# Attention and two expert layers on one core: the first expert of layer one chosen from two batches, its first two blocks in a fixed order, and an earlier split of the last w2 parts

## The chip, the cores and the metric

One core of a Trainium2 chip runs the kernel. The core has a matrix engine (TensorE, PE in the profile, with its weight loads as PEld), VectorE (DVE), ScalarE (ACT), GpSimd (POOL) and SyncE (SP). Each runs its own instructions in order and waits for the others on semaphores. SP issues the transfers of weights and the transposing transfers, POOL the gathers and scatters by a list of rows (SPq and POOLq in the profile are these issues). The metric is device time in microseconds (us).

## The reference, cut to what matters

The inputs are q, k, v of 4 batches, 12 heads, 448 tokens, head size 64. First comes causal attention; its output is laid out as 1792 rows of 768. Then two layers of 8 experts, each of which sends a token to one expert:

```python
scores = where(causal_mask, -1e9, scale * q @ k.T)
x = (softmax(scores) @ v).transpose(0, 2, 1, 3).reshape(1792, 768)
# layer one: router on normalised rows
logits = (x / norm(x)) @ (emb / norm(emb)).T / tau
e = argmax(logits); gate = softmax(logits)[e]
x = gate * (relu(x @ w1[e]) @ w2[e])          # w1[e]: 768 x 1024, w2[e]: 1024 x 768
# layer two: router with a bias by the token's modality
logits = x @ w_gate + modality_bias[modality_id]
e = argmax(logits); gate = softmax(logits)[e]
out = gate * (relu(x @ w1b[e]) @ w2b[e])
```

Counted by this reference on its own inputs (seed 0), layer one sends to its experts 0 to 7: [1 319 229 126 542 464 87 24] tokens in all, [0 54 217 121 1 41 0 14] of them in the first batch and [0 317 217 124 106 45 73 14] in the first two. Layer two sends [869 3 0 0 0 0 920 0].

## The kernel before, in words

**Attention.** A loop over 24 pairs of heads (`for g in range(NPR + 3)`) runs as a pipeline: in iteration g the scores and exponents of pair g, the halves of pair g-1 (two f16 parts, transposed by DMA into the tiles th and tl), the values and the output xb of pair g-2 (`values`, `combine`), and the router products of pair g-3 (`route_t` transposes xb on PE, `route_l` multiplies it with the embeddings). Six pairs make a batch. When a batch is through, its rows go to memory (`store_x`) and its routing runs piece by piece (`route1`, advanced by `tick`): logits, argmax, a token's slot among its expert's, the gate, and a scatter of the tokens' records (`meta1`).

**The experts.** A layer's tokens are worked off in blocks of 128 of one expert. A block gathers its records (`gather_m`, tile mg), its rows (`gather_x`, tile xg), turns x (`prep`), multiplies with w1 (`up`, two halves n=0 and 1), applies relu, turns h, multiplies with w2 (`down`), and scatters its output. All of it is float32 made of two parts, a high part (w1h, w2h, xh, hh, casts on ACT) and the rest (w1l, w2l, xl, hl, subtractions on DVE), with three products of parts for each: an up half is 18 matmuls 128x512, a down 24 pairs of 128x384. An expert's weights come as six w1 and eight w2 pieces (w1r, w2r) and are split by `split_w`. Layer one has 18 blocks and layer two 16 by the counts above. Experts are taken in an order that `Lead.order` makes of the counts; `table` makes the list of blocks, `switches` the list of the blocks at which the expert changes.

**The lead.** The first expert of layer one is chosen while attention still runs, so that its weights arrive and are split early: `choose(cnt1)` takes the expert with the most tokens so far. Before, this happens after batch 0 (expert 2, 217 tokens). `check` then sets flags: `full[0]`, at least 128 of its tokens are in the first two batches, so that block 0 can be gathered early, and `full[1]`, at least 256 in three batches, for block 1. `load_lead(m1, 1, c)` loads one piece of its w1 in each iteration from 18 on (`LEAD`). By the counts `full[0]` is set and `full[1]` is not.

**The opening of layer one.** `open_phase` and `first_block` run block 0 while the last batch's routing (`last_route1`) is finished in steps between the matmuls; then `run` works off the sections, j = 1 to 21, where section j holds up of block j and down of block j-1. Blocks 0, 1 and 2 turn x on PE (`prep`, j < FIRSTQ), later ones on DVE (`x_squares`, then `prep`). `warm` issues six matmuls whose result nobody reads, in front of the opening.

**The end.** In layer two block 15 is the last and the only one of its expert. After down of block 14, `split_w(2)` splits all eight w2 pieces of that expert, and `down_last` computes the two halves of the output, each sent away by itself.

The order of the instructions on every engine is that in which the Python program emits them; nothing reorders them later.

## Time and profile before

| | us |
|---|---|
| median of 3 timed runs | 921.35 |
| lowest and highest of them | 916.38, 922.5 |
| the profiled execution | 910.5 |
| its span in the trace | 908.7 |
| mean granted clock of TensorE, as a share of full speed | 0.98 |

All times in the trace count from the span's start. Attention's products end at 243.34, layer one's block 0 begins its up at 246.50, and section 3 (the first that works alike in both kernels) begins at 309.97. The last matmul is issued at 900.25. A row of a timeline gives the start and the duration of one instruction, or of several that follow one another (x6), the engine, the line in the program, the output and the inputs, and in brackets how long the engine stood idle before it and what released it. A matmul's duration contains its way through the pipeline: the next one starts earlier than this one ends.

### The profile page before, as it was taken

What the parts mean: (1) busy time and instruction counts of PE and PEld (TensorE: products, weight loads), DVE (VectorE), ACT (ScalarE), POOL (GpSimd) and SP (SyncE); (2) the same over time, 40 slices, a digit from 0 to 9 for tenths busy, and PEclk for the clock granted to TensorE, in tenths of its full rate; (3) what the DMA queues carried; (4) which work ended last, traced back from release to release, by engine and by line L of the source; (5) the groups of instructions that cost most, each with busy time, mean ns of one, the idle gap of its engine ahead of it and who ended that gap; (6) DMA issues with size and microseconds to landing.
All of it is one profiled execution on the core that took longest, in us unless ns stands there. A gap on an engine that the chain in (4) does not pass through costs nothing. (4 is left out here: it accounts for less than half of the span.)

```text
span 908.7 us, 21165 instructions
## 1 busy us (share of the span) xinstructions
PE 859.1 (95%) x7010; PEld 753.3 (83%) x7010; DVE 699.3 (77%) x1798; ACT 427.8 (47%) x779; POOL 478.0 (53%) x477
## 2 busy tenths in 40 slices
PE   4999999999789899999999999999999999999995
PEld 3877877877577899998898999888899898898984
DVE  7899999999785766787936884468886678976793
ACT  3676777767434664575525652245112133312323
POOL 7877577875255255454444564431653544544531
PEclk9999999999899999999999999999999999999998
DMA  6799996979717765578515662120281233511110
GB/s 193 161 154 171 203 181 159 210 172 218 241 53 254 278 257 176 203 282 296 193 38 183 201 231 97 53 76 6 57 332 39 67 88 133 185 48 54 54 38 16
DMA packets 114456, 137.46 MB, mean 151 GB/s; under 512 B 78382, under 2 KB 82788, under 8 KB 114289
## 3 DMA queue, kind: packets, MB, share of 16 engines
q1 hardware_dynamic: 101376, 108.76, 44.1%
q0 software_dynamic: 12912, 26.83, 9.4%
q8 instruction: 61, 1.00, 0.5%
q14 instruction: 107, 0.87, 0.3%
HBM read 101.48 MB, written 19.92 MB: 134 GB/s over the span
## 5 line engine op out<-in xcount | busy, mean ns | idle before, releaser
L765 POOL DMA_INDIRECT xg<-x,xi x128 | 137.7, 1076 | 98.3 <-DMA x<-yb,mg 50.8
L974 PE MATMUL h<-w1h,xh 128*128 128x512 f32 x408 | 165.0, 404 | 1.0 <-ACT xh L958 1.0
L976 PE MATMUL h<-w1h,xl 128*128 128x512 f32 x408 | 161.5, 396 | 1.0 <-DVE xl L959 1.0
L975 PE MATMUL h<-w1l,xh 128*128 128x512 f32 x408 | 161.3, 395 | 0.2 <-DVE w1l L715 0.2
L1039 PE MATMUL o<-w2h,hh 128*128 128x384 f32 x528 | 138.3, 343 | 0.2 <-ACT hh L988 0.2
L1039 PE MATMUL o<-w2h,hl 128*128 128x384 f32 x528 | 136.7, 340 | 0.9 <-DVE hl L989 0.9
L1039 PE MATMUL o<-w2l,hh 128*128 128x384 f32 x528 | 136.0, 339 | 0.1
L1016 DVE STREAM_TRANSPOSE hs<-h 32x256 f32<-32x256 f32 x240 | 107.0, 446 | 14.3 <-PE h L976 9.0
L435 ACT ACTIVATE ex<-sc,nm 112x112 f32<-112x112 f32 (+1 forms) x192 | 83.8, 503 | 62.2 <-DVE nm L430 60.9
L1039 PEld LDWEIGHTS o<-w2h,hl 128*128 128x128 f32 x528 | 96.4, 190 | 1.2 <-DVE hl L989 1.2
L1039 PEld LDWEIGHTS o<-w2l,hh 128*128 128x128 f32 x528 | 96.1, 189 | 0.7 <-DVEq L1330 0.4
L1039 PEld LDWEIGHTS o<-w2h,hh 128*128 128x128 f32 x528 | 94.8, 190 | 1.8 <-ACT hh L988 0.4
L976 PEld LDWEIGHTS h<-w1h,xl 128*128 128x128 f32 x408 | 77.3, 190 | 19.6 <-DVE xl L959 2.0
L1022 ACT ACTIVATE hh<-hs 128x512 fp32r<-128x512 f32 x30 | 18.4, 631 | 158.1 <-PE o L1039 88.6
L974 PEld LDWEIGHTS h<-w1h,xh 128*128 128x128 f32 x408 | 77.5, 190 | 16.6 <-ACT xh L958 1.1
L975 PEld LDWEIGHTS h<-w1l,xh 128*128 128x128 f32 x408 | 77.5, 190 | 16.2 <-DVE w1l L715 1.0
L715 DVE TENSOR_TENSOR w1l<-w1r,w1h 128x1024 fp32r<-128x1024 f32 x66 | 76.5, 1221 | 8.3 <-ACT w1h L713 7.5
L430 DVE TENSOR_REDUCE nm<-sc 112x1 f32<-112x112 f32 (+1 forms) x192 | 75.6, 439 | 6.1 <-PE sc L425 5.0
L715 DVE TENSOR_TENSOR w2l<-w2r,w2h 128x768 fp32r<-128x768 f32 x78 | 68.8, 953 | 8.2 <-ACT w2h L713 6.9
L713 ACT CAST w1h<-w1r 128x1024 fp32r<-128x1024 f32 x64 | 62.4, 1046 | 8.4 <-PE h L976 5.2
L947 DVE STREAM_TRANSPOSE xr<-xg 128x768 f32<-128x768 f32 x31 | 50.4, 1625 | 18.8 <-DMA xg<-x,xi 14.9
L713 ACT CAST w2h<-w2r 128x768 fp32r<-128x768 f32 x78 | 58.5, 849 | 0.6 <-ACTq L1421 0.6
(327 smaller groups left out, 1932.7 us busy)
## 6 DMA issues: line engine op xcount, KB each, us to landing
w1r<-in_w1a SPq DMA_DIRECT2D x48, 512.0 KB, 6.8
w2r<-in_w2a SPq DMA_DIRECT2D x64, 384.0 KB, 6.2
r<-in_kqP SPq DMA_DIRECT2D x24, 448.0 KB, 4.3
w1r<-in_w1b SPq DMA_DIRECT2D x18, 512.0 KB, 6.5
w2r<-in_w2b SPq DMA_DIRECT2D x24, 384.0 KB, 6.4
vr<-in_vh SPq DMA_DIRECT2D x24, 224.0 KB, 4.4
x<-xb SPq DMA_DIRECT2D x16, 336.0 KB, 4.3
xg<-x,xi POOLq DMA_INDIRECT x128, 3.3
```

The lines of the kernel that those rows point to most:

```text
L430: vec.tensor_reduce(out=nms[h][:, c : c + 1], in_=scs[h, c][:CP, : CP * (c + 1)], axis=AX.X, op=ALU.min)
L435: act.activation(dst, scs.pop((h, c))[:CP, :n], AF.Exp, bias=nms[h][:, c : c + 1], scale=-1.0)
L713: act.copy(hi[k], r[k])
L715: vec.tensor_sub(lo[k], r[k], hi[k].bitcast(F32))
L765: pool.indirect_dma_start(out=xgs[j % 3][:, q * (D // Q) : (q + 1) * (D // Q)], out_offset=None, in_=quarters, in_offset=IND(ap=xi[:, q : ...
L947: vec.transpose(xr.rearrange("p k (q r) -> p q k r", q=Q), xgs[j % 3].rearrange("p (q r k) -> p q k r", q=Q, k=KD))
L974: pe.matmul(hps, lhsT=xh[:, c], rhs=w1h[c][:, ns], start=(c == 0), stop=False)
L975: pe.matmul(hps, lhsT=xh[:, c], rhs=w1l[c][:, ns], start=False, stop=False)
L976: pe.matmul(hps, lhsT=xl[:, c], rhs=w1h[c][:, ns], start=False, stop=(c == KD - 1))
L1016: vec.transpose(hr[cols, :, rows], hps[rows, q * 256 : (q + 1) * 256].rearrange("p (c k) -> p k c", c=QR))
L1022: act.activation(hh[k], part, AF.Relu)
L1039: pe.matmul(ops[:, n, :384], lhsT=h[f // KH][:, f % KH], rhs=w[f][:, n * 384 : (n + 1) * 384], start=(f == 0 and st == 0), stop=(f == KF - ...
```

## The change

Layer one's lead is chosen from the counts of batches 0 and 1 together, and one flag is left: more than 256 of its tokens lie in these two batches. By the counts above that is expert 1 with 317. Block 0's gathers and block 1's records are fetched without a condition. Block 0's up is put into the end of attention (half 0 straight behind pair 22's router product), and half 1 is interleaved with the last batch's routing. If the flag is set, up and down of the first blocks follow in a fixed order (`open_first`); if not, `open_short` gathers again and computes blocks 0 and 1 again once the table is there. The `warm` matmuls are gone. Three of the six subtractions of w1 move from DVE to POOL (`psub`). The six w1 loads are put into iterations 20 to 23. Batch 1's routing begins an iteration earlier. The sections begin at j = 2. In layer two `split_last` splits three of the last expert's w2 pieces behind the matmuls of the down ahead, `x_squares` of the last blocks move into the section that uses them, and `down_last` has its second half in a bank of its own and evicts each half on ACT and DVE together. The diff, cut (`wb`, `wq` and the definitions that only move are left out):

```diff
+SOON = 3
+STOP = 2
-LEAD = 18
+LEAD = {20: (0,), 21: (1,), 22: (2, 3), 23: (4, 5)}
 # Lead.check
-                              op0=ALU.is_le if self.m == "m1" else ALU.is_lt)
+                              op0=ALU.is_lt)
 # route1_tail
+        if b == 1:
+            yield from lead1.choose(cnt1)
+            yield from lead1.check(cnt1, 0, 2)
...
-        if b == 0:
-            yield from lead1.choose(cnt1)
-        elif b == 1:
-            yield from lead1.check(cnt1, 0, 1)
-        elif b == 2:
-            yield from lead1.check(cnt1, 1, 2)
+        if b == B - 2:
+            yield STOP
 # the loop over pairs of heads
-        if g == NPR + 2:
-            warm(ps_T, "T", WV)
+        if g == NPR + 1:
+            split_w(1, (4, 5), ())
+            for k in range(3, KD):
+                psub(w1l[k], w1r[k], w1h[k].bitcast(F32))
...
-            route_t(r, xbs[r // PB])
+            if r == NPR - 1:
+                h0 = up(0, 0, {4: lambda: route_t(r, xbs[r // PB])})
+            else:
+                route_t(r, xbs[r // PB])
...
         if g == NPR + 1:
-            split_w(1, (4, 5), range(3))
-            warm(ps_T, "T", WV)
+            split_w(1, (), range(3))
+            prep(m1, 0)
...
-            for c in ((0,), (1,), (2,), (3,))[r % PB] if b < B - 2 else ((0, 1), (2, 3), (), ())[r % PB]:
+            for c in (((0,), (1,), (2,), (3,)), ((0,), (1,), (2, 3), ()), ((0, 1), (2, 3), (), ()))[b][r % PB]:
...
-        if LEAD <= g <= NPR:
-            for c in range(g - LEAD, KD if g == NPR else g - LEAD + 1):
-                load_lead(m1, 1, c)
+        for c in LEAD.get(g, ()):
+            load_lead(m1, 1, c)
...
         if g == NPR:
...
-            m1.gather_early((0,), 2 * S)
+            for j in range(2):
+                m1.gather_m(j, True)
+            m1.gather_x(0, 2 * S)
             load_lead(m1, 2)
-        if g == NPR + 2:
-            split_w(1, (), range(3, KD))
...
+    m1.gather_x(1, 2 * S)
+    drain(routing)
...
+    def open_first(m, h0):
+        relu(0, h0)
+        steps = last_route1()
+        split_w(2, range(KF), ())
...
+        h1 = up(0, 1, {2: turned_logits, 3: second_x, 5: lambda: next(steps)})
+        relu(1, h1)
+        next(steps)
+        m.gather_q(3)
+        ops = o_tile()
+        with tc.If(m.is_full() > 0) as full:
+            h0 = up(1, 0, {2: h_turn})
+            h_turned()
+            split_w(2, (), range(KF))
+            relu(0, h0)
+            h1 = up(1, 1)
+            relu(1, h1)
+            down(m, m.mg(0), between={4: lambda: prep(m, 2)}, late=ops)
+            load_next(m, m.second, 2)
+        with full.Else():
+            split_w(2, (), range(KF))
+            open_short(m, ops)
+        h_turn()
+        down_end(m, m.mg(0), ops)
+        h_turned()
 # the sections of a layer
+        def split_last(j):
+            with tc.If(nc.values_load(tab[0:1, 1, j : j + 1], engines=[ENG.Activation, ENG.DVE], min_val=0, max_val=1) > 0):
+                split_w(2, range(SOON), range(SOON))
...
-            near = m.routed and j >= NBLK - 1
+            near = j >= NBLK - 1
+            later = m.routed and j == 2
-            if FIRSTQ <= j + 1 < MAXB:
+            if j + 1 < MAXB and not later:
                 prep(m, j + 1, ra, MAXB if near and j >= NBLK else FIRSTQ + 1)
...
-                down(m, m.mg(j - 1), h_split)
+                down(m, m.mg(j - 1), lambda: (split_last(j) if near else None, h_split()))
...
-            for j in range(1 if m.routed else 2, MAXB):
+            for j in range(2, MAXB):
...
             with tc.If(cl > 0) as other:
-                split_w(2)
+                split_w(2, range(SOON, KF), range(SOON, KF))
 # down_last
-        ops = ps_a.tile([P, 2, 512], F32, tag="av", name="o")
+        ops = (o_tile()[:, 0], ps_h.tile([P, 512], F32, tag="h", name="o1"))
...
-            act.activation(yhs[n], ops[:, n, :384], AF.Copy, scale=mg[:, 2:3])
+            act.activation(yhs[n][:, :192], ops[n][:, :192], AF.Copy, scale=mg[:, 2:3])
+            vec.tensor_scalar_mul(yhs[n][:, 192:], ops[n][:, 192:384], mg[:, 2:3])
```

The order of PE where attention ends, before: `lg` is the router product of pairs 22 and 23, `tb` the transposes of pair 23's output, `t` those of the last logits, `xt` those of block 0's rows, `h` block 0's first up half.

```order
L531 MATMUL lg_4833<-xTl_5554,enT 16x448
L788 LDWEIGHTS ones
L788 MATMUL warm<-mask,ones 128x512
...
L518 MATMUL tb_275<-ident,xb_4385 128x112 x4
L530 MATMUL lg_4833<-xTh_5732,enT 16x448
L531 MATMUL lg_4833<-xTl_5733,enT 16x448
...
L1186 COMPARE_AND_BRANCH
L602 MATMUL t<-ident,lgs_5738 112x16 x4
L956 MATMUL xt<-ident,xg_338 128x128 x6
L974 MATMUL h<-w1h_5322,xh_5807 128x512
```

And now:

```order
L533 MATMUL lg_4820<-xTl_5550,enT 16x448
L836 MATMUL h<-w1h_5322,xh_5490 128x512
L837 MATMUL h<-w1l_5492,xh_5490 128x512
L838 MATMUL h<-w1h_5322,xl_5491 128x512
...
L838 MATMUL h<-w1h_5325,xl_5491 128x512
L520 MATMUL tb_275<-ident,xb_4373 128x112 x4
L836 MATMUL h<-w1h_5326,xh_5490 128x512
...
L838 MATMUL h<-w1h_5327,xl_5491 128x512
L532 MATMUL lg_4820<-xTh_5724,enT 16x448
L533 MATMUL lg_4820<-xTl_5725,enT 16x448
```

The first up half stands ahead of the last pair's transposes and around them, where the warm matmuls and the waits were; block 0's own x transposes have moved further ahead, in front of pair 23's values.

POOL at the same place, before: the two casts are parts of w1, `mg` and `xg` the gathers of block 0, `meta` the scatter of batch 2's records, `rt_sr` a root that the last batch's logits wait for.

```order
L164 TENSOR_SCALAR w1h_5322<-w1r_345 128x1024
L164 TENSOR_SCALAR w1h_5323<-w1r_346 128x1024
L771 TENSOR_LOAD ld_fullm_220
...
L746 DMA mg_339<-meta_63,ld_idxm_218 128x8
...
L749 DMA xg_338<-x_62,mg_339 128x768
...
L659 DMA meta_63<-mt_159,r1sir_5547 14336x8
...
L174 TENSOR_TENSOR rt_sr_5726<-r1ss_5557,half 112x4
```

And now:

```order
L166 TENSOR_SCALAR w1h_5323<-w1r_346 128x1024
L751 DMA mg_339<-meta_63,ld_idxm_218 128x8
L751 DMA mg_340<-meta_63,ld_idxm_218 128x8
L754 DMA xg_338<-x_62,mg_339 128x768
L169 TENSOR_TENSOR w1l_5495<-w1r_348,w1h_5325 128x1024
L169 TENSOR_TENSOR w1l_5496<-w1r_349,w1h_5326 128x1024
L169 TENSOR_TENSOR w1l_5497<-w1r_350,w1h_5327 128x1024
L176 TENSOR_TENSOR rt_sr_5705<-r1ss_5553,half 112x4
L754 DMA xg_5752<-x_62,mg_340 128x768
L663 MEMSET pad 128x1
L664 DMA meta_63<-mt_159,r1sir_5538 14336x8
```

The three subtractions of w1 stand between the gather of block 0's rows and the root, and block 1's gather (`xg_5752`) stands behind the root and ahead of batch 2's scatter.

DVE behind the last up of layer two, before: `hs` are the squares of h, `hl` its low part, `w2l` the last expert's w2.

```order
L1016 STREAM_TRANSPOSE hs<-h 32x8x32 x16
L1023 SCALAR_TENSOR_TENSOR hl_5794<-hs,hh_5796 128x512
L1023 SCALAR_TENSOR_TENSOR hl_5795<-hs,hh_5797 128x512
L1409 COPY gt<-mg_341 128x8
L1421 UNCONDITIONAL_BRANCH x8
L1433 COMPARE_AND_BRANCH
L715 TENSOR_TENSOR w2l_5799<-w2r_5496,w2h_5801 128x768
```

And now:

```order
L876 STREAM_TRANSPOSE hs<-h 32x8x32 x16
L1230 TENSOR_LOAD t_tabm_333
L1230 COMPARE_AND_BRANCH
L720 TENSOR_TENSOR w2l_5803<-w2r_5498,w2h_5805 128x768
L720 TENSOR_TENSOR w2l_5804<-w2r_5499,w2h_5806 128x768
L720 TENSOR_TENSOR w2l_5773<-w2r_5500,w2h_5807 128x768
L1230 UNCONDITIONAL_BRANCH x2
L883 SCALAR_TENSOR_TENSOR hl_5798<-hs,hh_5800 128x512
L883 SCALAR_TENSOR_TENSOR hl_5799<-hs,hh_5801 128x512
L1289 COPY gt<-mg_341 128x8
```

Three of the eight subtractions have moved ahead of h's low part and of the branch.

## Rows read from the trace of the kernel before

**Rows 1.** The page: busy time of each engine, share of the span, instructions.

```profile
PE 859.1 (95%) x7010; PEld 753.3 (83%) x7010; DVE 699.3 (77%) x1798; ACT 427.8 (47%) x779; POOL 478.0 (53%) x477
```

**Rows 2.** Windows of 50 us; columns as in the first line.

```profile
core 0: us, PE busy (x) PEld busy (x) DVE busy (x) ACT busy (x) POOL busy (x), PEclk, DMA share, GB/s
200.00:250.00 50.00, 42.47 (x662) 33.54 (x659) 43.31 (x135) 31.64 (x66) 18.65 (x25) 0.88 0.89 222
250.00:300.00 50.00, 43.71 (x209) 35.29 (x209) 34.32 (x102) 20.36 (x33) 28.84 (x31) 0.94 0.53 177
```

**Rows 3.** Waits of PE after 310 us, the longest: total, times, longest.

```profile
PE o L1067 <- ACT w2h L713: 2.8, 1, 2.8
```

**Rows 4.** Timeline of PE, 225 to 310 us: start, duration, operation, [idle before <-releaser].

```profile
225.21 0.24 PE L490 MATMUL av<-vr,tl 112*128 112x64 bf16 x1 [0.39 <-DMA tl<-al]
...
238.19 1.47 PE L788 MATMUL warm<-mask,ones 112*128 112x512 bf16 x6
...
241.07 0.60 PE L518 MATMUL tb<-ident,xb 112*128 112x112 f32 x4 [1.42 <-DVE xb L509]
...
248.66 0.79 PE L976 MATMUL h<-w1h,xl 128*128 128x512 f32 x1 [0.97 <-DVE xl L959]
...
278.41 0.47 PE L974 MATMUL h<-w1h,xh 128*128 128x512 f32 x1
...
282.39 0.39 PE L976 MATMUL h<-w1h,xl 128*128 128x512 f32 x1
...
298.62 0.17 PE L1116 MATMUL pr<-ob,triu 128*128 128x8 bf16 x1 [2.23 <-DVE ob L1109]
...
309.62 0.51 PE L1039 MATMUL o<-w2h,hl 128*128 128x384 f32 x2
309.97 0.40 PE L974 MATMUL h<-w1h,xh 128*128 128x512 f32 x1
```

**Rows 5.** Window with the w1 load ahead of pair 22's transposes; columns as in rows 2.

```profile
222.00:225.00 3.00, 1.60 (x15) 1.34 (x15) 2.79 (x12) 2.46 (x5) 0.21 (x2) 0.89 1.05 290
```

**Rows 6.** One window in block 0's first up half; columns as in rows 2.

```profile
249.26:251.39 2.13, 2.13 (x7) 1.65 (x5) 2.10 (x17) 0.00 (x0) 0.00 (x0) 0.50 0.01 4
```

**Rows 7.** Timeline of DVE around 189 us, and of its w1 part.

```profile
188.98 2.04 DVE L217 TENSOR_TENSOR am_ohr<-r1lgr,am_mxr 112x32 f32<-112x32 f32 x1
190.94 0.84 DVE L448 SCALAR_TENSOR_TENSOR al<-ex,ah 112x672 f16<-112x672 f32 x1
...
234.65 3.49 DVE L715 TENSOR_TENSOR w1l<-w1r,w1h 128x1024 fp32r<-128x1024 f32 x3
```

**Rows 8.** Groups of POOL by form: count, busy us, mean ns, idle before.

```profile
L167 POOL TENSOR_TENSOR lo<-r,hi 128x896 fp32r<-128x896 f32 x22 | 47.3, 2150 | 1.8
```

**Rows 9.** Timeline of POOL around 189 us.

```profile
188.88 2.08 POOL L167 TENSOR_TENSOR lo<-r,hi 128x896 fp32r<-128x896 f32 x1
190.93 1.76 POOL L167 TENSOR_TENSOR r<-vr 112x512 f32<-112x512 f32 x1
```

**Rows 10.** Timeline of POOL: gathers of x, block 0 (early), block 1.

```profile
221.15 0.95 POOL L749 DMA_INDIRECT xg<-x,mg  x1 [2.40 <-DMA mg<-meta,ld_idxm]
...
265.02 1.42 POOL L749 DMA_INDIRECT xg<-x,mg  x1 [0.30 <-issue]
```

**Rows 11.** Timeline of ACT in block 0.

```profile
254.61 3.03 ACT L713 CAST w2h<-w2r 128x768 fp32r<-128x768 f32 x4
```

**Rows 12.** Timeline of DVE, last two sections and the end.

```profile
882.50 1.62 DVE L947 STREAM_TRANSPOSE xr<-xg 128x768 f32<-128x768 f32 x1
...
887.69 7.04 DVE L715 TENSOR_TENSOR w2l<-w2r,w2h 128x768 fp32r<-128x768 f32 x8 [1.57 <-ACT w2h L713]
```

**Rows 13.** Timeline of PE, down of the last block.

```profile
887.71 0.44 PE L1067 MATMUL o<-w2h,hh 128*128 128x384 f32 x1 [2.78 <-ACT w2h L713]
...
896.12 0.44 PE L1067 MATMUL o<-w2h,hh 128*128 128x384 f32 x1 [0.72 <-ACT yb L1069]
...
900.25 0.34 PE L1067 MATMUL o<-w2h,hl 128*128 128x384 f32 x1
```

More of the change, by code (lines that the diff above doesn't have):

```diff
@@ L688, in tick @@
         for _ in range(1 if g < NPR else 6):
-            if routing is not None and (first or not hold):
-                hold = next(routing, None) == ALIGN
+            if routing is not None and hold != STOP and (first or hold != ALIGN):
+                hold = next(routing, None)
     def both(fn, g, *a, ticks=True):
@@ new lines, in attention_two_moe_kernel @@
+    b = B - 1
+    for c in range(NCH):
+        store_x(b, c)
+    st_v.close()
+    tb.clear()
+    ps_a = left("ps_a", 1, space=PSUM)
+    wq = left("wq", 1)
+    xgs += [wq.tile([P, D], F32, name=f"xg{i}") for i in range(1, 3)]
+    m1.gather_x(1, 2 * S)
+    drain(routing)
+    xr = wq.tile([P, KD, P], F32, name="xr")
+    yb = wq.tile([P, D], F32, name="yb")
+    yT = wq.tile([P, KD, P], F32, name="yT")
+    w2_part = lambda t, k: wq.tile([P, D], F32R, name=f"w2{t}{k}")
+    x_1 = x_split(wq, 1)
```

382 lines of the change are left out of this document (181 added, 201 removed).

## The prediction

> **What bounds the kernel now.** I read the page first, then PE by windows, then PE's waits, then its timeline where the windows are not full. The page says that PE is busy for 859.1 us of a span of 908.7 [rows 1], so a change can win at most the rest, and only where PE stands still or runs at its lower clock. The windows of 50 us show where that is: 42.47 of 50 busy at a granted clock of 0.88 between 200 and 250, and 43.71 at 0.94 between 250 and 300 [rows 2]. That is the end of attention and the opening of layer one. Behind 310 us the longest wait of PE is 2.8 us [rows 3], at the last block. So the change works on the two places that have anything to give. The opening is the larger: the six warm matmuls start at 238.19 when pair 22's router product is issued, and section 3 starts at 309.97 [rows 4]. Those 71.8 us are the measure of the main term.
>
> The sum is made against the profiled execution (910.5 us, span 908.7). It lies 1.2% below the median of the timed runs, 921.35, and below the fastest, 916.38. I carry the gain over in microseconds and subtract it from the median.
>
> **Term A, two w1 loads ahead of a pair's transposes.** The last iterations now issue two 512 KB pieces of w1 each instead of one, on SP, ahead of the transposing transfers of pairs 22 and 23 (the moves of x stores and routing by an iteration come with them). In the window in which one such piece goes ahead of pair 22's transposes the transfers are full: share 1.05, 290 GB/s [rows 5]. A second piece takes 524 KB / 290 GB/s = 1.8 us, and PE already waits for this transpose today, 0.39 us [rows 4]. I take +1.8: one of the two iterations pays in full, since nothing covers it. The upper end is +4 (both pay 1.8, and the DMA is slower by a little), the lower -2 (two iterations earlier on issue no load now, and batch 2's routing steps come in other places).
>
> **Term B, the opening.** The work that PE must do between pair 22's router product and section 3 is the same in both kernels but for the warm matmuls: six up halves, two downs, and small products. An up half at full clock goes from 278.41 to 282.39 for its first and last start, and one more spacing of 0.23: 4.2 us [rows 4]. A down is 24 pairs at 309.97 - 309.62 = 0.35 us, 8.4 us [rows 4]. That is 6 x 4.2 + 2 x 8.4 = 42 us. The 42 transposes of x (12), h (24) and y (6) I estimate at 0.15 us each, by the four of `tb` that take 0.60 [rows 4]: 6.3, and with the last pair's transposes and the router products 7. Necessary is 49; spent are 71.8. So 22.8 us are waits, warm matmuls (1.47), branches and lower clock. Single waits of it: 1.42 for xb, 0.97 for xl, 2.23 for ob [rows 4]; and in block 0's first up half five matmuls take 2.13 us at a granted clock of 0.50, which is TensorE's 1.2 GHz level, instead of 5 x 0.23 = 1.2 [rows 6].
>
> What is left of the 22.8 in the new order, wait by wait:
> - Third matmul of the first up half waits for xl. DVE does three w1 subtractions (3.49 us [rows 7]) before xl. It starts them at 234.65, is through at 238.2 and has xl 1.0 later; PE wants it at 238.7. Without more that is 0.5; POOL adds to it. POOL now subtracts three 128x1024 pieces beside DVE; by its 128x896 subtraction of 2150 ns [rows 8] one takes 2.46. At 189 us a DVE operation on 112x32 with two operands takes 2.04 us, more than half of what three of 128x1024 take, while a POOL subtraction of 2.08 runs, and both end together [rows 7, 9]: one holds the other off. I add half a POOL piece, 1.2: 1.7 in all. Ends: 0.5, and 0.5 + 2.46 = 3.0 for a whole piece.
> - Block 1's x. On POOL its gather stands behind the three subtractions and the root, which itself waits for DVE's last row sums. PE gets pair 23's xb at 241.07 today [rows 4]; xl and POOL's pieces put it about 2 later, and row sums and root I estimate at 1 us each, so POOL is through about 245.3. The gather's issue takes 0.95, and its landing is an estimate of 3 us, from 2.40 for the records' gather [rows 10]. PE wants it about 247.5 and gets it about 249.3: 1.8 (ends 0 and 4).
> - xh of block 1 stands behind all eight w2 casts on ACT, 8 x 0.76 = 6.1 us [rows 11]: 1.2 (ends 0 and 3).
> - down of block 0 needs w2l, which DVE does behind the table: 1.5 (ends 0 and 3). Nearest row: today's 0.97 for xl [rows 4].
> - Block 2's x: its gather comes behind eight scatters and the table: 1.9 (ends 0 and 4). Nearest row: 2.23 for ob [rows 4].
> - After such a wait the clock falls again: one stretch like that one, twice as long: 2 (ends 0 and 4).
>
> That is 10.1 of the 22.8, so B is -12.7. The single ends hardly all come together; by half of them to either side I take -18 and -6. The eight w2 casts and the eight w2 subtractions cost nothing of themselves: they lie beside PE's up halves, and where that cover is gone the two waits above are the price. Section j = 1 disappears, but its matmuls are in the count above. The new order of the experts moves switches between blocks of one expert; PE has no wait for weights behind 310 us today [rows 3], the singles (experts 0, 7, 6, 3) are the same, so I cost it at nothing.
>
> **Term C, the end.** DVE's last eight w2 subtractions take 7.04 us and run from 887.69 to 894.73, PE waits 2.78 us before, and the second half of the output waits 0.72 for the eviction of the first [rows 12, 13]. Now three of them, 3 x 0.88 = 2.6, come ahead of hl and fill time in which DVE did an x transposition of 1.62 us for a block that does not exist [rows 12]; that one goes, another moves from section 13 into 14. Five are left behind the branch, 4.4 us, and begin no earlier than 887.7 to 888.8, since ACT does their casts behind the branch and DVE passes two more branches: end at 892.2 to 893.2, a gain of 1.5 to 2.5. The own bank takes off the 0.72. The eviction in two parts gives some 0.2. The second half itself still takes 900.25 - 896.12 = 4.1 us [rows 13]. I take -2.5, ends -0.5 (hl late by its own order) and -3.7.
>
> **The sum** is 1.8 - 12.7 - 2.5 = -13.4 us, so a span of about 895.3 and a median of 921.35 - 13.4 = 907.9.
>
> **The rivals.**
> 1. POOL and DVE take turns. In the two timelines around 189 us [rows 7, 9] DVE, once held off, gets two operations through (am_ohr, then al at 190.94) before POOL's next. If instead each of DVE's three w1 subtractions and its small two-operand steps waits for one POOL piece, xl and the last pair's xb come later by one or two further pieces, 2.6 us here: 910.5. For it: one instance is thin evidence. Against it: that instance. The Trainium skill (SBUF — State Buffer, "SBUF: two separate sides") says that the port pair that VectorE and GpSimd share is an exclusive lock, taken for a whole instruction by whichever starts first, and that a VectorE operation with two SBUF inputs needs it. By that rule alone, with POOL's pieces queued back to back, this rival would hold; the trace's 2.04 us agrees with the lock, the order behind it is open.
> 2. The opening's waits are only renamed. The waits of term B come to 17 instead of 10, since xh, w2l and block 2's x are all one behind the other and each drop of the clock costs again. B is then -6, the sum 1.8 - 6 - 2.5 = -6.7: 914.7, within 1%. For it: DVE is busy for 34.32 of 50 and ACT for 20.36 between 250 and 300 [rows 2], and the chain from the last logits through the table to block 2's gather is not shorter than before. Against it: two blocks' ups now lie beside this chain, where one did.
> 3. The other way: the stretch at the lower clock stays away, since PE has no gap ahead of block 0, and the DMA costs nothing. B is -17, A is 0: 921.35 - 19.5 = 901.9.
> 4. Slower: the flag is not set. Then the Else branch gathers and computes blocks 0 and 1 again, behind the table. Decisive is whether the lead has more than 256 tokens in two batches. Its first gather of x would land about 269.4 (block 1's, behind the table, does so today by its issue at 265.02 [rows 10], 1.42 and the estimated 3), and block 0's up would begin there instead of at 246.50: +22.9, A and C as above: 921.35 + 22.9 + 1.8 - 2.5 = 943.6. For it: nothing in the trace, which knows only the old flag. Against it: the counts, 317.
>
> **How the numbers follow.** A measurement of this kernel can tell about 1%, 9.2 us, from no change. Chances: the forecast as it stands, 902 to 912.5, 0.52; rival 1 on top 0.12; rival 3 0.11; rival 2 0.20; rival 4 0.03; the rest, 0.02, something slower that I do not name. Faster by over 1% (below 912.1) takes the forecast, rival 1 and rival 3, less a little of their upper ends: 0.74. Within 1%: rival 2 and those ends, 0.21. Slower 0.05. The range 897 to 917 takes in rivals 1 to 3 and half of the ends of terms A and C; it leaves out rival 4, the unnamed case, the upper part of rival 2 and the lower part of rival 3.
>
> **What would show it.** Of A: PE's wait for the low halves' transposes of pairs 22 and 23, about 2 us instead of 0.39. Of B: the first up half starting within 0.3 us of pair 22's router product; the waits of its third matmul for xl (1.7), of block 1's transposes for the gather (1.8), of block 1's up for xh (1.2), of block 0's down for w2l (1.5), of block 2's transposes for the gather (1.9); section 3 starting near 299.1 (309.97 + 1.8 - 12.7); granted clock above 0.9 in the windows from 240 to 300. For rival 1: DVE's w1 subtractions lasting over 2 us each. For rival 4: up of block 0 twice in the timeline. Of C: three w2 subtractions ahead of hl, the last one ending about 881.7 (892.6 less the 10.9 won before it), and no wait of the second half for an eviction. I am wrong if section 3 starts later than 305, or if waits for weights appear behind it.

## The result and the profile after

| | before | changed |
|---|---|---|
| median of 16 timed runs each, us | 921.04 | 926.02 |
| lowest and highest | 911.42, 930.24 | 921.05, 931.22 |
| ratio, with its 95% interval | | 1.0084 [1.0057, 1.011] |
| the profiled execution, and its span | 910.5, 908.7 | 923.55, 921.8 |

The forecast was 907.9 us, a gain of 13.4. Measured is a loss of 0.84% of 921, that is 7.7 us [5.2, 10.1]; the two medians alone lie 5.0 us apart. By the 1% that the prediction named as what can be told from no change, this is still "within 1%", to which it gave 0.21, but for another reason (rival 2).

The page of the changed kernel, its line of engines (busy us, share of the span, instructions), against [rows 1]:

```profile
PE 855.5 (93%) x6998; PEld 753.6 (82%) x6998; DVE 703.2 (76%) x1791; ACT 427.8 (46%) x779; POOL 485.1 (53%) x480
```

PE has 3.6 us less work than before and a span that is 13.1 longer. So PE stands still for 16.7 us more. The windows of the changed kernel, in 50 us (columns as in the first line), say where:

```profile
core 0: us, PE busy (x) PEld busy (x) DVE busy (x) ACT busy (x) POOL busy (x), PEclk, DMA share, GB/s
150.00:200.00 50.00, 42.89 (x714) 35.16 (x713) 47.34 (x109) 30.61 (x68) 44.98 (x40) 0.97 0.85 161
200.00:250.00 50.00, 41.65 (x728) 34.44 (x724) 43.79 (x110) 35.14 (x74) 28.24 (x24) 0.93 0.91 206
250.00:300.00 50.00, 38.20 (x179) 31.05 (x179) 25.17 (x96) 12.40 (x23) 22.98 (x30) 0.93 0.56 195
```

Beside [rows 2], 250 to 300 lost 5.5 us of PE's work instead of winning any (the opening begins 9 us later in it). And 150 to 200 is a place of which the prediction did not speak. The same stretch in the kernel before:

```profile
150.00:200.00 50.00, 47.91 (x824) 39.53 (x821) 49.02 (x133) 37.37 (x83) 43.80 (x40) 0.97 0.90 189
```

Four marks that both traces have cut the difference: pair 22's router product (before 237.77, after 246.83), section 3's first product (309.97 [rows 4], 319.56), the first product of down(14) (876.42, 888.76), and the span's end.

| stretch | before | after | difference | forecast |
|---|---|---|---|---|
| attention, to pair 22's router product | 237.77 | 246.83 | +9.06 | A: +1.8 |
| opening, to section 3 | 72.20 | 72.73 | +0.53 | B: -12.7 |
| sections 3 to 14 | 566.45 | 569.20 | +2.75 | 0 |
| end, from down(14) | 32.28 | 33.04 | +0.76 | C: -2.5 |

(The prediction counted the opening from the first warm matmul, 238.19, which gave 71.8.)

**Attention.** The timeline of the changed kernel, POOL at 140 us (start, duration, operation, idle before and its releaser):

```profile
139.93 0.10 POOL L663 MEMSET pad<- 128x1 f32 x1
150.28 1.20 POOL L664 DMA_INDIRECT meta<-mt,r1sir  x1 [10.25 <-DVE rinv L503]
```

And the same scatter in the kernel before:

```profile
145.97 0.10 POOL L658 MEMSET pad<- 128x1 f32 x1
151.78 1.21 POOL L659 DMA_INDIRECT meta<-mt,r1sir  x1 [5.70 <-DVE ld_onem L217]
```

It is the first scatter of batch 0's records (`route1_tail`). Before, the steps that choose the lead stood between this batch's gates and its scatters. The changed kernel chooses after batch 1, so these steps are gone from there, and the scatter stands a pair earlier in POOL's order, while the slots that it needs come from DVE no earlier. POOL, which works in order, stands for 10.25 us instead of 5.70, and behind it are the subtractions for the coming pairs. It then has to catch up. The windows 160 to 180, of the kernel before, then of the changed one:

```profile
160.00:180.00 20.00, 19.96 (x368) 16.83 (x368) 19.72 (x46) 16.61 (x38) 17.16 (x17) 1.00 1.11 217
```

```profile
160.00:180.00 20.00, 15.30 (x276) 12.76 (x277) 17.81 (x36) 11.91 (x27) 18.89 (x18) 1.00 0.96 200
```

POOL is busy for 18.89 of 20 and PE loses 4.7. One instance of what POOL's catching up does to DVE, the changed kernel's timelines of POOL and of DVE:

```profile
172.50 2.11 POOL L169 TENSOR_TENSOR lo<-r,hi 128x896 fp32r<-128x896 f32 x1
```

```profile
172.56 2.77 DVE L450 SCALAR_TENSOR_TENSOR al<-ex,ah 112x672 f16<-112x672 f32 x1
```

`al` takes 0.84 alone [rows 7]. Here it ends at 175.33, 0.72 us behind the end of the POOL subtraction (174.61), as if most of it ran only then. The Trainium skill (SBUF — State Buffer, "SBUF: two separate sides") calls the port pair that the two engines share an exclusive lock. This instance, 2.77 us for 0.84, agrees.

**The opening.** PE's timeline in the changed kernel, the rows with a wait (idle before, releaser, in brackets), and section 3's first row:

```profile
248.13 0.49 PE L837 MATMUL h<-w1l,xh 128*128 128x512 f32 x1 [0.49 <-DVE w1l L720]
250.87 0.50 PE L838 MATMUL h<-w1h,xl 128*128 128x512 f32 x1 [2.24 <-DVE xl L821]
260.89 1.04 PE L818 MATMUL xt<-ident,xg 128*128 128x128 f32 x6 [1.06 <-DMA xg<-x,mg]
264.79 0.47 PE L836 MATMUL h<-w1h,xh 128*128 128x512 f32 x1 [0.53 <-ACT xh L820]
275.30 0.62 PE L899 MATMUL o<-w2l,hh 128*128 128x384 f32 x2 [0.75 <-DVE w2l L720]
280.80 1.04 PE L818 MATMUL xt<-ident,xg 128*128 128x128 f32 x6 [1.38 <-DMA xg<-x,mg]
288.82 0.38 PE L860 MATMUL ht<-ident,hs 128*128 128x128 f32 x2 [2.14 <-issue]
302.04 1.54 PE L940 MATMUL yt<-ident,yb 128*128 128x128 f32 x6 [7.11 <-DVE hl L868]
...
319.56 0.48 PE L836 MATMUL h<-w1h,xh 128*128 128x512 f32 x1
```

The first six are the waits of term B (the first two together its wait for xl); all lie within the ends that it gave them, two at half their size or less. The last two were in no list. The 2.14 before 288.82 is released by nothing but issue, six transposes behind the place where PE leaves the If over its Else; what the time goes to, no run shows. Both waits cost twice, since the granted clock behind each is 0.50, the 1.2 GHz level (windows of the changed kernel):

```profile
289.80:292.80 3.00, 3.00 (x9) 2.30 (x7) 0.00 (x0) 0.00 (x0) 2.27 (x3) 0.50 1.02 387
302.00:306.70 4.70, 4.66 (x14) 3.89 (x15) 3.53 (x18) 1.46 (x3) 3.47 (x6) 0.50 0.24 88
```

What the 7.11 waits for stands in the changed kernel's timelines of ACT, DVE, POOL and SP:

```profile
299.73 1.05 ACT L908 ACTIVATE yb<-o,mg 128x384 f32<-128x384 f32 x2 [17.38 <-DMA mg<-meta,t_idxm]
```

```profile
299.72 0.17 DVE L912 COPY ym<-mg 128x8 f32<-128x8 f32 x1 [16.70 <-DMA mg<-meta,t_idxm]
```

```profile
289.15 1.00 POOL L770 DMA_INDIRECT xg<-x,xi  x1 [0.35 <-POOL xi L766]
...
301.06 1.02 POOL L913 DMA_INDIRECT x<-yb,mg  x1 [7.13 <-ACT yb L908]
```

```profile
280.30 3.37 SPq L707 DMA_DIRECT2D w1r<-in_w1a  x6
286.11 8.72 SPq L707 DMA_DIRECT2D w2r<-in_w2a  x8
```

Block 0's last product is issued at 285.50. Its eviction (ACT) and the copy of its records (DVE) stand behind the If, and both read mg0, which the Else would gather anew. So both wait until POOL is past the end of the If, at 299.7 (join and in_branch below show that it is this). POOL has block 3's quarter gathers ahead of it, issued from 289.15 to 293.9, and the second expert's weights fill the transfers just then (385 GB/s, share 1.01 between 285.6 and 288.8). h of block 1 waits in the same line behind the eviction, so PE has nothing to do.

**The end.** DVE in the changed kernel, from the last section on, against [rows 12]:

```profile
887.44 1.60 DVE L809 STREAM_TRANSPOSE xr<-xg 128x768 f32<-128x768 f32 x1 [1.61 <-DVEq L1210]
...
890.91 3.65 DVE L876 STREAM_TRANSPOSE hs<-h 32x256 f32<-32x256 f32 x8
895.09 3.67 DVE L876 STREAM_TRANSPOSE hs<-h 32x256 f32<-32x256 f32 x8 [0.53 <-issue]
898.79 2.69 DVE L720 TENSOR_TENSOR w2l<-w2r,w2h 128x768 fp32r<-128x768 f32 x3
901.40 1.29 DVE L883 SCALAR_TENSOR_TENSOR hl<-hs,hh 128x512 fp32r<-128x512 f32 x2
...
903.87 4.43 DVE L720 TENSOR_TENSOR w2l<-w2r,w2h 128x768 fp32r<-128x768 f32 x5 [1.10 <-ACT w2h L718]
```

And PE's last down there, against [rows 13]:

```profile
901.07 0.69 PE L927 MATMUL o<-w2h,hh 128*128 128x384 f32 x1 [3.79 <-ACTq L1299]
902.89 0.69 PE L927 MATMUL o<-w2l,hh 128*128 128x384 f32 x1 [1.13 <-DVEq L1299]
909.07 0.34 PE L927 MATMUL o<-w2h,hh 128*128 128x384 f32 x1
```

The three early subtractions are there, and the second half no longer waits for the eviction (909.07 has no bracket). The copy of block 15's x has moved from section 13 into 14 (it stands at 865.92), as forecast. But by the same edit the copy for block 16, a block that does not exist, has moved from the end of section 14 to the front of section 15. It (887.44) and its xl now come in front of section 15's h copies, 3.5 us from 887.44 to 890.91. So h, the early subtractions and hl come later, PE waits 3.79 instead of 2.78, and starts at half clock.

**Sections 3 to 14.** PE's waits of over 0.5 us between section 4 and down(14) of the changed kernel:

```profile
385.08 1.47 PE L940 MATMUL yt<-ident,yb 128*128 128x128 f32 x6 [1.41 <-DVE hl L868]
...
427.78 1.12 PE L940 MATMUL yt<-ident,yb 128*128 128x128 f32 x6 [1.42 <-DVE hl L868]
...
622.35 0.84 PE L940 MATMUL yt<-ident,yb 128*128 128x128 f32 x6 [1.34 <-DVEq L1299]
...
665.46 0.47 PE L836 MATMUL h<-w1h,xh 128*128 128x512 f32 x1 [1.47 <-issue]
```

The kernel before has two there, 1.41 at 414.21 and 1.40 at 609.00, both of `yt` too. 5.64 in all instead of 2.81 accounts for the 2.75. Two of the four waits are new, and they are of two kinds. The one at 385.08 comes behind a section in which DVE splits both the w2 of one expert and the w1 of the next, in front of hl (DVE of the changed kernel):

```profile
366.42 7.07 DVE L720 TENSOR_TENSOR w2l<-w2r,w2h 128x768 fp32r<-128x768 f32 x8 [0.33 <-ACT w2h L718]
375.97 6.91 DVE L720 TENSOR_TENSOR w1l<-w1r,w1h 128x1024 fp32r<-128x1024 f32 x6 [0.34 <-issue]
```

Between 310 and 600 both fall into one section twice in the changed kernel (sections 5 and 7) and once in the kernel before (section 7), and a wait of `yt` follows each time. In section 5 it is the two-block expert 2, which was the lead before and now has blocks 4 and 5. The wait at 665.46 has nothing to do with the order: it stands before PE's first product behind the If of layer two's opening (`open_next`). All seven kernels with the changed opening have it, with 0.98 to 1.82 us, and none of the five with the old one. Why, no run shows.

### The profile page after: what moved, and what is told of

Read it like the earlier page. It is cut to its first block, busy times and chain, and to the rows that moved or that the text cites. A ratio compares the mean times of both kernels' runs of the same rounds, so it can differ in the third digit from the quotient of the medians.

```text
span 921.8 us, 21126 instructions
## 1 busy us (share of the span) xinstructions
PE 855.5 (93%) x6998; PEld 753.6 (82%) x6998; DVE 703.2 (76%) x1791; ACT 427.8 (46%) x779; POOL 485.1 (53%) x480
## 5 line engine op out<-in xcount | busy, mean ns | idle before, releaser
L770 POOL DMA_INDIRECT xg<-x,xi x128 | 136.7, 1068 | 95.5 <-DMA x<-yb,mg 53.6
L899 PEld LDWEIGHTS o<-w2h,hl 128*128 128x128 f32 x528 | 95.4, 188 | 0.0
L720 DVE TENSOR_TENSOR w1l<-w1r,w1h 128x1024 fp32r<-128x1024 f32 x63 | 74.3, 1247 | 2.6 <-issue 2.2
L809 DVE STREAM_TRANSPOSE xr<-xg 128x768 f32<-128x768 f32 x30 | 48.3, 1611 | 16.9 <-DMA xg<-x,xi 8.9
```

The costliest lines, as they stand in the source:

```text
L720: vec.tensor_sub(lo[k], r[k], hi[k].bitcast(F32))
L770: pool.indirect_dma_start(out=xgs[j % 3][:, q * (D // Q) : (q + 1) * (D // Q)], out_offset=None, in_=quarters, in_offset=IND(ap=xi[:, q : ...
L809: vec.transpose(xr.rearrange("p k (q r) -> p q k r", q=Q), xgs[j % 3].rearrange("p (q r k) -> p q k r", q=Q, k=KD))
L899: pe.matmul(ops[:, n, :384], lhsT=h[f // KH][:, f % KH], rhs=w[f][:, n * 384 : (n + 1) * 384], start=(f == 0 and st == 0), stop=(f == KF - ...
```

## The experiments

Ten kernels ran, in three groups that each have runs of the kernel before beside them. That kernel's median moved from group to group (914.39, 917.86, 914.07), so only ratios within a group compare. Beside the times the table has five readings of each trace: from DVE's `rinv` of pair 12 to that of pair 22 (attention's part behind the scatters), POOL's wait before the first scatter, from pair 22's router product to section 3 and to section 4, and from down(14) to the end.

| kernel | median | ratio [95%] | pairs 12 to 22 | POOL's wait | to section 3 | to section 4 | end |
|---|---|---|---|---|---|---|---|
| before | 921.04 | 1 | 89.7 | 5.70 | 72.2 | 91.6 | 32.3 |
| changed | 926.02 | 1.0084 [1.0057, 1.011] | 97.8 | 10.25 | 72.7 | 92.4 | 33.0 |
| before_again | 917.5, one run | | 95.4 | 5.70 | 72.3 | 91.7 | 32.3 |
| b_early | 913.0 | 0.997 [0.9933, 1.0007] | 91.4 | 5.70 | 72.0 | 91.4 | 32.3 |
| join | 925.23 | 1.0113 [1.0043, 1.0183] | 97.7 | 10.25 | 63.2 | 92.5 | 33.5 |
| tail_old | 922.1 | 1.0078 [1.0045, 1.0111] | 98.3 | 10.25 | 71.8 | 91.4 | 32.3 |
| in_branch | 924.56 | 1.0084 [1.0043, 1.0124] | 102.7 | 11.58 | 61.6 | 87.6 | 33.1 |
| wait7 | 923.76 | 1.0065 [1.0035, 1.0095] | 93.9 | 5.70 | 68.6 | 88.2 | 32.8 |
| b_scatter | 920.68 | 1.004 [1.0006, 1.0074] | 96.7 | 10.25 | 71.4 | 90.8 | 32.3 |
| all3 | 918.5 | 0.9994 [0.9964, 1.0025] | 92.4 | 5.69 | 63.0 | 88.4 | 30.2 |
| b_tail | 914.42 | 1.000 [0.9966, 1.0035] | 88.9 | 5.70 | 76.1 | 95.5 | 31.0 |
| all4 | 914.5 | 0.9984 [0.9949, 1.002] | 93.3 | 5.70 | 62.3 | 87.2 | 30.1 |

**before_again**: the kernel before, unedited, for the scatter of its own trace.

> The kernel before, once more, for a second trace. Its first profiled execution took 910.5, below every timed run then shown, and its timed runs spread from 911.4 to 930.2. Theory C: attention's length varies between executions; pair 22's router product comes 5 to 10 us later than 237.8 here, with a span near 918. Theory E: 237.8 plus or minus 2 and a span near 909.

Its attention part took 95.4 us where the first profile had 89.7. The opening and the end repeat within 0.1. So attention varies by some 6 us from one execution to the next, and the first profile was a short one: 910.5 against a median of 921. Of the 9.06 us in the table of stretches a part is no effect of the change.

**b_early**: the kernel before, with batch 1's rows stored and routed an iteration earlier, as the change does it.

```diff
-            for c in ((0,), (1,), (2,), (3,))[r % PB] if b < B - 2 else ((0, 1), (2, 3), (), ())[r % PB]:
+            for c in (((0,), (1,), (2,), (3,)), ((0,), (1,), (2, 3), ()), ((0, 1), (2, 3), (), ()))[b][r % PB]:
```

> The kernel before with batch 1's rows stored and its routing begun an iteration earlier, as the change does; the lead is chosen after batch 0 as before. Theory E: this alone makes attention longer, since POOL's scatters of batch 0 come in a row and its parts of the pairs then fall on DVE's operations with two operands: pair 22's router product 5 to 10 us later than 237.8, and 0.4 to 0.9% slower. Rival C (the length of attention depends on how POOL and DVE happen to meet, in any kernel): within 2 us of the sample of the kernel before that runs beside it, or no order between them. Rival L (the w1 loads): no difference from before.

91.4 us and 0.997: the earlier routing of batch 1 slows nothing. My first theory for the loss in attention fell here.

**b_scatter**: the kernel before, with the lead's choice put behind batch 0's scatters. The scatters thereby come as early in POOL's order as in the changed kernel, and nothing else changes.

```diff
-        if b == 0:
-            yield from lead1.choose(cnt1)
-        elif b == 1:
+        if b == 1:
...
+        if b == 0:
+            yield from lead1.choose(cnt1)
```

> The kernel before with only this: the lead's choice after batch 0 comes behind the scatters of batch 0 instead of ahead of them, so that POOL reaches the first scatter one pair earlier, as in the change. Theory P: POOL waits about 10 us there, pair 12's to pair 22's output takes 95 to 99 us, and the kernel is 0.4 to 0.9% slower than before. Rival: 89 to 92 and no difference.

POOL's timeline in that kernel:

```profile
147.97 1.20 POOL L657 DMA_INDIRECT meta<-mt,r1sir  x1 [10.25 <-DVE rinv L501]
```

The same wait of 10.25, 96.7 us, and 0.4% slower (3.7 us, interval 0.6 to 6.8): this order alone makes the kernel before slower. The lower end of that interval is close to nothing, and 96.7 is only 1.3 above the longest part with the old order.

**wait7**: the changed kernel with seven empty steps ahead of batch 0's scatters.

```diff
+        if b == 0:
+            for _ in range(7):
+                yield
```

> The changed kernel with seven empty steps ahead of the scatters of batch 0, where the choice of the lead stood before: POOL's first scatter moves behind pair 14's halves again. In the three executions with the changed attention POOL waits 10.25 us at this scatter for DVE, and from pair 12's output to pair 22's it takes 97.7 to 98.3 us, against 89.7, 95.4 and 91.4 in three with the old one. Theory P: POOL's wait, which holds up its parts of the next pairs, makes the difference: here 89 to 93.5, POOL's wait 6 or less. Rival: the wait costs nothing by itself, 97 or more.

POOL's timeline in that kernel:

```profile
151.08 1.20 POOL L667 DMA_INDIRECT meta<-mt,r1sir  x1 [5.70 <-DVE rinv L505]
```

The wait is 5.70 again and the part takes 93.9, just outside the 93.5 that I gave. Over all traces: 88.9 to 95.4 us with the wait of 5.70 (seven traces, mean 92.1), 96.7 to 102.7 with 10.25 or 11.58 (five traces, mean 98.6). The two sets do not overlap. The times are less sharp: 1.0065 against the 1.0084 of the changed kernel fits a return of 3.7 us and one of nothing. The opening is shorter here as well, by 4.1 us, though no edit touches it: PE waits 0.28 for xl (2.24 in the changed kernel). So the changed opening varies from trace to trace too.

**join**: the changed kernel with block 3's quarter gathers behind the end of the If.

```diff
-        m.gather_q(3)
         ops = o_tile()
         with tc.If(m.is_full() > 0) as full:
...
         h_turned()
+        m.gather_q(3)
```

> The changed kernel with one line moved: block 3's quarter gathers (gather_q(3)) stand behind the end of the If of the opening instead of ahead of it. Theory J: in the changed kernel ACT's output yb and DVE's copy ym of block 0 wait until POOL has passed the end of that If, and POOL gets there only after its four quarter gathers have landed behind the second expert's weights (yb at 299.72, 14 us behind the last matmul of down). Then yb begins here within 5 us of down's last matmul, PE's wait of 7.1 us at yt is below 1, the lower clock behind it goes as well, and section 3 starts 7 to 10 us earlier measured from pair 22's router product (72.7 us in the changed kernel). Theory F (fetching of code past the long Else branch stops all engines, as PE's 2.14 us shows): yb stays 10 us or more behind down, and the 72.7 stay within 2.

The 7.11 is gone, section 3 comes after 63.2 us. But section 4 comes after 92.5, as late as in the changed kernel. PE and DVE in join's section 3:

```profile
324.02 1.51 PE L940 MATMUL yt<-ident,yb 128*128 128x128 f32 x6 [3.90 <-DVE hl L868]
```

```profile
308.94 1.64 DVE L809 STREAM_TRANSPOSE xr<-xg 128x768 f32<-128x768 f32 x1 [9.66 <-DMA xg<-x,xi]
```

Block 3's x is late now, and behind it on DVE are w1's subtractions (PE waits 0.39 and five times 0.17 for them) and block 4's x, another 2.43 late at 321.76.

**in_branch**: the changed kernel with `down_end` in both branches, so that nothing behind the If reads mg0.

```diff
             down(m, m.mg(0), between={4: lambda: prep(m, 2)}, late=ops)
+            down_end(m, m.mg(0), ops)
             load_next(m, m.second, 2)
...
             open_short(m, ops)
+            down_end(m, m.mg(0), ops)
         h_turn()
-        down_end(m, m.mg(0), ops)
```

> The changed kernel with the output step of block 0 (down_end: ACT's yb, DVE's copy ym, POOL's scatter) written inside both branches of the opening's If instead of behind it; block 3's gathers stay where they were. Moving those gathers behind the If instead took 9.6 us off the opening and gave 7.6 back in section 3, which then waited for block 3's x and the second expert's w1. Theory J: yb waits for nothing but the matmuls once it is in the branch (286.2 instead of 299.7 in the changed kernel's time), PE's 7.1 us wait at yt goes with its lower clock, and from pair 22's router product to section 3 it is 62 to 65 us instead of 72.7, with section 3 as in the changed kernel: 0.7 to 1.1% faster than that. Rival W: section 3 waits again by as much, since the second expert's weights are what is late; then the last matmul comes at most 3 us earlier.

ACT in in_branch:

```profile
290.42 1.05 ACT L908 ACTIVATE yb<-o,mg 128x384 f32<-128x384 f32 x2 [3.69 <-PE o L899]
```

The eviction now waits for PE alone, with the quarter gathers where they were. That shows the wait to be the If's end. Section 3 comes after 61.6 us; DVE in it:

```profile
321.45 1.54 DVE L809 STREAM_TRANSPOSE xr<-xg 128x768 f32<-128x768 f32 x1 [6.00 <-DMA xg<-x,xi]
```

Block 4's x is 6.00 late, hl stands behind it, PE waits 4.46 for that at 323.70, and of 11 us won 6 are given back: 87.6 to section 4, 4.8 less than the changed kernel. The times show none of it, 1.0084 like the changed kernel, where I expected 0.7 to 1.1% less. Its attention took 102.7 us in the trace, the longest of all; but the changed kernel has POOL's long wait too, so that does not tell where the 4.8 went.

**tail_old**: the changed kernel with the old end.

```diff
-            near = j >= NBLK - 1
+            near = m.routed and j >= NBLK - 1
...
-                down(m, m.mg(j - 1), lambda: (split_last(j) if near else None, h_split()))
+                down(m, m.mg(j - 1), h_split)
...
-                split_w(2, range(SOON, KF), range(SOON, KF))
+                split_w(2)
```

(with one bank and one eviction by ACT in `down_last`, as before).

> The changed kernel with the end of layer two as before: all eight w2 parts split behind the branch, x squares of the last blocks ahead, one bank for both halves, eviction on ACT alone. From the first matmul of down of block 14 to the end of the span it was 32.3 us before and is 33.0 in the changed kernel. Theory: the moved x squares stand in front of DVE's h squares and eat up what the three early splits win; then this kernel has 32.3 plus or minus 0.5 and the same time as the changed one within 0.2%. Rival (the early splits are worth their 2.5 us and something else at the end costs): 34.5 or more. Its attention and opening are those of the changed kernel: a second sample of both, 246.8 and 72.7 if they do not depend on chance.

32.3 us again: the changed end is worse by 0.7, not better.

**all3**: in_branch's and wait7's edits together, and the changed end with the last blocks' x copies where the kernel before has them.

```diff
-            near = j >= NBLK - 1
+            near = j >= (NBLK - 1 if m.routed else NBLK + 1)
...
-                prep(m, j + 1, ra, MAXB if near and j >= NBLK else FIRSTQ + 1)
+                prep(m, j + 1, ra, MAXB if near and j >= (NBLK if m.routed else NBLK + 2) else FIRSTQ + 1)
...
-                down(m, m.mg(j - 1), lambda: (split_last(j) if near else None, h_split()))
+                down(m, m.mg(j - 1), lambda: (split_last(j) if j >= NBLK - 1 else None, h_split()))
```

> The changed kernel with three repairs: down_end in the branches, seven empty steps ahead of batch 0's scatters, and x squares of layer two's last blocks ahead as before (only the two for blocks that cannot exist dropped), with the early splits and the own bank kept. If all three theories hold: attention 89 to 94 from pair 12 to 22, the opening 62 to 65, and 29 to 31 us from the first matmul of down of block 14 to the end (32.3 before, 33.0 changed), in all 1 to 1.8% faster than before. If the weights of the second expert are what is late, faster than before by less than 0.5%.

Each of the three shows: 5.69, 63.0, and an end of 30.2 us, 2.1 below the kernel before. DVE at all3's end has no copy of x between 882.30 and the splits:

```profile
882.30 0.96 DVE L831 TENSOR_TENSOR xl<-xr,xh 128x768 fp32r<-128x768 f32 x1 [0.83 <-DVEq L1214]
883.27 3.65 DVE L879 STREAM_TRANSPOSE hs<-h 32x256 f32<-32x256 f32 x8
...
891.15 2.70 DVE L723 TENSOR_TENSOR w2l<-w2r,w2h 128x768 fp32r<-128x768 f32 x3
```

The whole is 0.57% faster than wait7 beside it by the medians, and equal to the kernel before; the 1 to 1.8% did not come. Against the first trace of the kernel before, the opening's gain to section 4 is 3.2 us, the end's 2.1, and the sections behind take back about 3.

Two comparisons within this group say more. in_branch and all3 differ by the seven steps and the end alone: 1.0084 [1.0043, 1.0124] against 0.9994 [0.9964, 1.0025], 8.3 us by the ratios and 6.1 by the medians, of which the end gives 2.9 in the traces. That leaves some 3 to 5 us for POOL's wait. wait7 keeps the wait for the If's end (8.25 us before `yt`), and comes to section 4 after 88.2 us, as early as all3 with 88.4. So the 3.2 is not shown to be the branch's: the changed opening as it stands took 92.4, 91.4 and 88.2 us to section 4 (changed, tail_old, wait7), with `down_end` in the branches 87.6, 88.4 and 87.2 (in_branch, all3, all4).

**b_tail**: the kernel before with the early splits, the own bank and the shared eviction alone, its x copies untouched.

> The kernel before, unchanged but for its end: three of the last expert's w2 parts are split behind the down ahead's products, the last down's second half has a bank of its own and its eviction is shared by ACT and DVE; the two x copies that the changed kernel draws in front of DVE's h squares stay where the kernel before has them (its row of DVE 882.50 us). Theory T (the prediction's term C is right and only the moved x copies spoil it in the changed kernel): from the first product of down(14) to the span's end 30.2 us in place of 32.3, all else as in the kernel before; the total 0.2% shorter, 0.9975 to 1.000 of it. Rival M (the copies are not to blame; the early splits or the bank are): 33.0 us there as in the changed kernel, 1.001.

31.0 us at the end, a gain of 1.3 where I expected 2.1. The expectation was careless. This kernel still does the copy for block 17, which does not exist, right in front of the splits; its DVE:

```profile
884.09 1.62 DVE L948 STREAM_TRANSPOSE xr<-xg 128x768 f32<-128x768 f32 x1
885.60 2.68 DVE L716 TENSOR_TENSOR w2l<-w2r,w2h 128x768 fp32r<-128x768 f32 x3
```

1.3 us are 0.14%, too little for its interval. Its opening (76.1 to section 3) is longer than the kernel before's without an edit there; PE waits 5.56 for `ob` where [rows 4] have 2.23. So the opening varies too.

**all4**: all3 with the gathers of blocks 4 and 5 in the branch, behind `down_end`.

```diff
             down_end(m, m.mg(0), ops)
+            m.gather_m(5)
+            m.gather_r(5)
+            m.gather_q(4)
             load_next(m, m.second, 2)
```

(the same in the Else; in `run` they are taken out, and the table of the Else is one that nothing behind the If reads).

> The run with all three mends (seven empty steps ahead of batch 0's scatters, down_end in both branches of the opening's If, the x copies of the last blocks ahead), and besides: the mg and quarter gathers of blocks 5 and 4 (gather_m(5), gather_r(5), gather_q(4)) are issued in the branch, right behind down_end, in place of behind the If and in section 2; and the table that the Else writes is not the one that the switches behind the If write. Theory L (what that run gave back in section 3, an wait of 3.71 us for block 4's x behind DVE's wait of 6.85 us for the quarter gathers, is their late issue behind POOL's wait at the If's end): section 4 begins 84 to 86 us after pair 22's router product, where the run with the three mends had 88.4 and the kernel before 91.6; the total 0.993 to 0.997 of the kernel before. Rival D (the gathers land late because the second expert's weights hold the DMA engines, whenever they are issued): section 4 at 88 us as before, the total 0.997 to 1.002.

87.2 to section 4, nearer to D's 88 than to L's 84 to 86, and the total of 0.9984 is outside L's too. But D's reason does not hold for block 4's x. DVE in all4:

```profile
298.94 1.54 DVE L813 STREAM_TRANSPOSE xr<-xg 128x768 f32<-128x768 f32 x1 [13.29 <-DMA xg<-x,xi]
...
309.15 1.57 DVE L813 STREAM_TRANSPOSE xr<-xg 128x768 f32<-128x768 f32 x1
```

Block 4's x is there in time now (309.15 has no wait). Block 3's x comes 58.9 us after pair 22's router product, where all3 had 51.6, although its gathers were issued at the same distance (43.3 and 42.4). Its tile is one that the Else writes too, and POOL gets past the If later with three more gathers in front of the end. That it is the same wait as `yb`'s is my reading; no run takes it away by itself. By the times all4 is no better than the kernel before.

## Why the prediction was wrong

**Term A (+1.8)** named the wrong place. PE's waits for the low halves' transposes are no larger than without the change: 1.7 us for `tl` in three pieces between 200 and 250, where before_again has 2.6 in one. And the loss begins before 200, while the changed kernel's first w1 load is issued at 207.45. The step that failed is the half-sentence that batch 2's routing "come[s] in other places", priced with the w1 loads and bounded only by a gain. It was batch 0's routing, and POOL's order was not followed where something had been taken out ahead of a waiting instruction. Its price is 3.7 us [0.6, 6.8] by b_scatter's times, 3 to 5 by those of in_branch and all3, 6.5 by the traces' means.

**Term B (-12.7)** failed in its list of waits, not in their sizes. Section 3 began at 319.56, behind the 305 from which the prediction called itself wrong. The six listed came to 0.49 + 2.24 for xl (1.7 forecast), 1.06 (1.8), 0.53 (1.2), 0.75 (1.5), 1.38 (1.9), and 1.4 for the half clock from 252.2 to 255 (2): 7.9 in place of 10.1. The list had no line for the end of the If and the place behind it: 2.14 for PE's issue, 1.5 for 3 us at half clock behind it, 7.11 for `yb`, and 2.35 for 4.7 us at half clock behind that, 13.1 in all. The 49 us of work were also some 3 too few, since 72.7 - 7.9 - 13.1 leaves 51.7. Without the If's end the opening is shorter by 9 to 11 (join, in_branch, all3), near the -12.7. But most of that is lost one section later (all of it in join, over half in in_branch and all3), where block 4's x is the next thing that is late; and wait7, with the If's end as it was, is at section 4 as early as all3. Section 3 was the wrong mark to stop the sum at, and what the If's end costs the whole kernel stays open.

**The order of the experts (0)** cost 1.4 us, one more wait of `yt`; the other 1.5 of the 2.75 stand behind layer two's If, of which the prediction has no word. I looked at the experts of one block, which are the same and follow each other alike in both orders, and not at the one of two blocks. That the order is the cause is read from the traces (all seven changed kernels have this wait, none of the five others); no run undoes it alone.

**Term C (-2.5)**: the forecast's mechanism gives -2.1 when the copies of x stay where they were (all3). The copy that I had "move from section 13 into 14" did so. What I did not follow is that the next one, for a block that does not exist, moves from section 14 into 15 with it; there it came in front of the h copies and turned -2.1 into +0.8.

**The sum.** b_scatter's 3.7, the opening's 0.5, 2.8 in sections 3 to 14 and 0.8 at the end make 7.8, and the times say 7.7 [5.2, 10.1]. That they agree so closely is chance, as the 3.7 alone is uncertain by 3. The traces' 13.1 has the first profile's short attention in it. I had carried that profile as an offset of 1.2%, and took for attention's normal course what was a good draw.

**The rivals.** Rival 2, waits renamed, was the nearest in kind, though the new wait was none of those that it named. Rival 1's lock shows in attention (`al`, 2.77 for 0.84). In the opening each of POOL's three pieces, from 239.98 to 247.00, held up one DVE instruction: one on 112x32 took 1.46 us (0.19 before), a cast on 112x4 took 2.05 (0.17), and the first w1 subtraction 2.94, where the other two took 1.21. So the engines took turns there, as rival 1 has it; but only one w1 subtraction met a piece, and PE's wait for xl, 2.73, stayed within the term's ends (0.5 and 3.0). Rivals 3 and 4 did not come; up of block 0 runs once. No rival had the slower side for a reason in POOL's queue.

## What to carry to other kernels

When steps are taken out of an in-order queue, look at what moves up: an instruction that still waits for the same data now blocks its queue longer. Look at code behind a branch that reads what either branch writes: here it waited for the slowest engine through that branch, with the transfers that this engine had under way, and finishing the work inside the branch took the wait away. And carry a forecast gain one stage further than the stage that wins it, to the first transfer that the faster stage does not move.

## What the runs showed of the hardware

- Just behind the If of layer one's opening, which PE leaves over its Else, PE stood 1.87 to 2.64 us with nothing but issue as releaser (2.14, 2.21, 2.27, 2.35, 2.02, 1.87 and 2.64 in the changed kernel, join, in_branch, all3, wait7, all4 and tail_old). Behind layer two's If it was 0.98 to 1.82 in the same kernels, and nothing in the five with the old opening, which have that If too. So leaving an If has no fixed price here, and its cause is not shown.
- A stall of 7.11 us of PE was followed by 4.7 us at a granted clock of 0.50, the 1.2 GHz level, and one of 2.14 by 3 us. After 3.79 at the end it was 0.50 from 901 to 907.
- Three POOL subtractions on 128x1024, one behind the other, each held up one DVE instruction beside them, whatever its size: 1.46, 2.05 and 2.94 us for what takes 0.19, 0.17 and 1.21.
- The same attention took between 88.9 and 95.4 us for ten pairs in executions with the same instruction order there, as much as most edits in this study were worth.
